# A fused attention and SoLU kernel: the row maximum by an accumulating multiply, the low half of x on VectorE, a group's first value product later

## The chip, the cores and the metric

The kernel runs on one core of one Trainium2 chip. The metric is the device time of one execution in microseconds (us), the median of several runs. TensorE (PE) multiplies matrices, VectorE (DVE), ScalarE (ACT) and GpSimd (POOL) work element by element, and SyncE (SP) issues most transfers. TensorE's results lie in PSUM, which GpSimd does not touch in this kernel.

## What is computed

```python
kv_flat = kv.reshape(B, H//4, 4, W//4, 4, C).mean(axis=(2, 4)).reshape(B, -1, C) @ w_sr   # k = v
s = q @ k.T / sqrt(C); a = softmax(s)              # 4 x 12288 queries, 768 keys, C = 128
x = a @ v                                          # 49152 tokens of 128
h = x @ w_in                                       # 1024 wide
u = h * softmax(h)
out = ((u - mean(u)) / sqrt(var(u) + 1e-6) * g_ln) @ w_out
```

Products are made as three products of split operands (a high half, and a low half that holds what the high half lost), so `x`, `k`, `v`, `q`, `u` and the weights all exist as two tiles each.

## The kernel before

The 49152 tokens are 384 **tiles** of 128; four tiles are a **group** (96 of them), and 96 tiles share one batch's keys. The main loop (L762) runs over slots. In slot `s` it works on the scores of tile `s`, on the hidden layer of tile `s-10` and `s-11`, and on the output product of tile `s-13`. From slot 9 on the order of instructions is written by hand: each engine executes its instructions in the order in which the loop emits them.

In one slot, in that order: `scores_exp` (L379: VectorE takes the negated maximum of the 768 scores in PSUM, ScalarE makes the exponential in place and then the high half `phl`), `hidden_u` (L499: VectorE, `u = h * rz * e` with an accumulated sum), the first part of `values` (one product `xa += v * pT`, L423), `scores_pe` of the next tile (L359, six products), GpSimd's steps, `hidden_var` on ScalarE, `hidden_max` and `hidden_bias` (L471 to L482: VectorE's negated maximum of the 1024 elements of `h`, then a multiply of this one column by the tile's `rz`), `hidden_exp` (L484: ScalarE, which needs that column), the rest of `values`, `scores_split` (L392: VectorE makes the low half of `phl`, and SyncE issues its transposing transfer into `pT`), `hidden_pe` (L460, six products into `h`), `final_pe` (L544, 24 products from `uT`), `hidden_turn` (L524: SyncE issues the transposing transfer of `u`'s halves into `uT`).

Three PSUM tiles (`ps_r`, L78) go round between scores and hidden tiles. The scores of the next tile take over the tile that `hidden_u` read, and `hidden_pe` takes over the tile that `scores_split` read in the same slot. One PSUM bank (`ps_x`, L79) holds `xa`, the value product of a whole group.

Once a group: 18 value products are spread over four slots (`values`, L405, shares 4, 5, 5, 4; in slots where a batch's key work needs TensorE, and in the slots of the same place in every batch, 0, 6, 6, 6). Then `values_out` (L427) lets ScalarE copy `xa` out twice, as 16 bits (`xh`) and as four bytes (`xf`). In the next slot, which is called slot 1 of the group below, `values_split` (L436) lets GpSimd subtract the two into `xl`, `values_norm` (L442) prepares the softmax sums on GpSimd, `values_recip` (L451) makes `rz` from them, and `final_out` (L574) writes an earlier group's result. GpSimd also splits `u` for every tile (L520, L521), and in most slots of batches 0 to 2 it adds up the next batch's keys (`kv_add`, L190, L201).

Of the kernel before, what the change touches and what calls it, by code (L numbers as in the profile page):

```python
# [11 lines left out]
F32 = mybir.dt.float32  # L12
F32R = mybir.dt.float32r
F16 = mybir.dt.float16
# [7 lines left out]
P = 128  # L22
# [9 lines left out]
GT = 4  # L32
# [20 lines left out]
def kernel(  # L53
# [70 lines left out]
    def kv_alloc(b):  # L124
        for n, w, dt, bufs in (
            ("kT", NK, F32, 1),
            ("ks", NK, F32, 1),
            ("kh", NK, F32R, 2),
            ("kl", NK, F32R, 2),
            ("ksq", NK, BF16, 1),  # L130
            ("kss", 2, F32, 1),
            ("knm", 2, F32, 1),
            ("vf", NK, F32, 1),
            ("sv", 2, F32, 2),
            ("bb", 4, F32, 2),
        ):
            state[n, b] = bat.tile([P, w], dt, tag=n, name=f"{n}_{b}", bufs=bufs)
        for n in ("vh", "vl"):
            state[n, b] = bat.tile([P, NKC, P], F16, tag=n, name=f"{n}_{b}")
# [125 lines left out]
    def kv_bound(b, part):  # L265

        knm, bb, sv = state["knm", b], state["bb", b], state["sv", b]  # L270
        if part == 0:
            nc.vector.tensor_tensor(knm[:, 0:1], knm[:, 0:1], knm[:, 1:2], op=ALU.max)
            nc.vector.tensor_scalar(
                bb[:, 0:1], knm[:, 0:1], wmax2, 1e-20, op0=ALU.mult, op1=ALU.max
            )
            nc.vector.tensor_scalar(knm[:, 0:1], knm[:, 0:1], 1e-28, None, op0=ALU.max)
            nc.gpsimd.tensor_tensor(bb[:, 0:1], bb[:, 0:1], mhalf[:, 0:1], op=ALU.pow)
            nc.gpsimd.tensor_tensor(knm[:, 0:1], knm[:, 0:1], mhalf[:, 0:1], op=ALU.pow)
        elif part == 1:
            nc.vector.tensor_scalar(  # L280
                bb[:, 1:2], bb[:, 0:1], SC * 1e-3 * 2.0**15, None, op0=ALU.mult
            )
            nc.vector.tensor_scalar(bb[:, 0:1], bb[:, 0:1], SC, None, op0=ALU.mult)
            nc.vector.tensor_scalar(bb[:, 2:3], bb[:, 1:2], 1e-9, None, op0=ALU.mult)
            pow2_under(knm[:, 0:1])
        else:
            nc.vector.tensor_scalar(knm[:, 0:1], knm[:, 0:1], 2.0**5, None, op0=ALU.mult)
            nc.vector.tensor_scalar(bb[:, 3:4], knm[:, 0:1], wsc, None, op0=ALU.mult)
            nc.vector.tensor_scalar(sv[:, 1:2], sv[:, 1:2], knm[:, 0:1], None, op0=ALU.mult)

    def kv_vs(b, half):
# [113 lines left out]
    def values(g, qtr, part):  # L405
        share = {0: [0, 0, 18, 0], 1: [0, 6, 6, 6]}.get(g, [4, 5, 5, 4])
        first = GT * g + GT - 1 + LAV
        if g > 1 and {first % TPB, first % TPB + TPB} & WITH_PE:
            share = [0, 6, 6, 6]
        s0 = sum(share[:qtr])  # L410
        s1 = s0 + share[qtr]
        if s0 == s1:
            return
        s0, s1 = ((s0, s0 + 1), (s0 + 1, s1))[part]
        b = g * GT // TPB
        if s0 == 0:
            state["xa", g] = ps_x.tile([P, 512], F32, tag="x", name=f"xa_{g}")
        xa, pT = state["xa", g], state["pT", g]
        vh, vl = state["vh", b], state["vl", b]
        seq = [(a, c, v) for c in range(NKC) for (a, v) in ((0, vh), (1, vh), (0, vl))]  # L420
        for n in range(s0, s1):
            a, c, v = seq[n]
            nc.tensor.matmul(  # L423
                xa, v[:, c, :], pT[:, :, a * NKC + c, :], start=n == 0, stop=n == len(seq) - 1
            )

    def values_out(g):  # L427
        b = g * GT // TPB
        xa, sv = state.pop(("xa", g)), state["sv", b][:, 1:2]
        xf = grp.tile([P, 512], F32, tag="xf", name=f"xf_{g}", bufs=1)  # L430
        xh = grp.tile([P, 512], F16, tag="xh", name=f"xh_{g}")
        nc.scalar.activation(xh, xa, AF.Copy, scale=sv)
        nc.scalar.activation(xf, xa, AF.Copy, scale=sv)
        state["xf", g] = (xf, xh)

    def values_split(g):  # L436
        xf, xh = state.pop(("xf", g))
        xl = grp.tile([P, 512], F16, tag="xl", name=f"xl_{g}")
        nc.gpsimd.tensor_tensor(xl, xf, xh, op=ALU.subtract)  # L439
        state["x", g] = (xh, xl)  # L440

    def values_norm(g):  # L442
        b = g * GT // TPB
        zz = grp.tile([P, GT], F32, tag="zz", name=f"zz_{g}", bufs=2)
        rz = grp.tile([P, 2, GT], F32, tag="rz", name=f"rz_{g}", bufs=3)
        nc.gpsimd.tensor_scalar(  # L446
            zz, state.pop(("z", g)), 1e-9, state["bb", b][:, 3:4], op0=ALU.add, op1=ALU.mult
        )
        state["zz", g] = (zz, rz)

    def values_recip(g):  # L451
        zz, rz = state.pop(("zz", g))
        nc.vector.reciprocal(rz[:, 0, :], zz)
        nc.scalar.activation(rz[:, 1, :], rz[:, 0, :], AF.Copy, scale=state["bb", g * GT // TPB][:, 0:1])  # L454
        state["rz", g] = (rz[:, 0, :], rz[:, 1, :])
        state["z2", g] = grp.tile([P, GT], F32, tag="z2", name=f"z2_{g}", bufs=3)
        state["v3", g] = grp.tile([P, GT], F32, tag="v3", name=f"v3_{g}", bufs=3)

# [10 lines left out]
        state["h", t] = h  # L469

    def hidden_max(t):  # L471
        g, j = divmod(t, GT)
        nm = wrk.tile([P, 2], F32, tag="nm2", name=f"nm2_{t}", bufs=3)
        nc.vector.tensor_reduce(nm[:, 0:1], state["h", t], axis=AX.X, op=ALU.max, negate=True)  # L474
        state["nm", t] = nm

    def hidden_bias(t):
        g, j = divmod(t, GT)
        nm = state["nm", t]
        nc.vector.tensor_scalar(  # L480
            nm[:, 1:2], nm[:, 0:1], state["rz", g][0][:, j : j + 1], None, op0=ALU.mult
        )  # L482

    def hidden_exp(t):  # L484
        g, j = divmod(t, GT)
# [4 lines left out]
            e,  # L490
            state["h", t],
            AF.Exp,
            bias=nm[:, 1:2],
            scale=state["rz", g][0][:, js],
            accum_out=state["z2", g][:, js],
        )
# [2 lines left out]
    def hidden_u(t):  # L499
# [3 lines left out]
        nc.vector.scalar_tensor_tensor(  # L503
            u,
            state.pop(("h", t)),
            state["rz", g][1][:, j : j + 1],
            state.pop(("e", t)),
            op0=ALU.mult,
            op1=ALU.mult,
# [239 lines left out]
    def at(t, fn, *args):  # L749
        if 0 <= t < NT:  # L750
            fn(t, *args)

    def at_last(t, fn, *args):

        if 0 <= t < NT and t % GT == GT - 1:
            fn(t // GT, *args)
# [5 lines left out]
    for slot in range(NT + LO + 2):  # L762
# [16 lines left out]
                st[0]()  # L779
        at(slot, scores_exp)  # L780
        at(i - 1, hidden_u)
        if 0 <= av < NG:
            values(av, qtr, 0)
        at(slot + 1, scores_pe)
        at_last(slot - NORM, values_norm)
        at_last(slot - XSP - 1, values_split)
        at_last(slot - FSC, final_scale)
        if slot < NT and 0 < qs < slot and (slot - 1 - qs) % GT == 0:
            q_low(slot // GT + 1)
        at(i - 1, hidden_split)  # L790
        at(i - 1, hidden_var)
        at(i, hidden_max)
        at(i, hidden_bias)
        at(i, hidden_exp)
        for f in fill.get(slot, []):
            f()
# [7 lines left out]
                f()  # L804
        at(slot, scores_split)
        at_last(slot - NORM, values_recip)
        at(i + 1, hidden_pe)
        at(slot - LO, final_pe)
        at(i - 1, hidden_turn)
# [43 lines left out]
```

## Time and profile before

| | us |
|---|---|
| median of 3 runs | 1930.72 |
| lowest, highest | 1929.51, 1938.44 |
| profiled execution | 1927.93 |
| its span | 1926.1 |
| PE busy | 1855.6 |
| ACT busy | 1803.2 |
| DVE busy | 1795.2 |
| POOL busy | 1705.3 |

An engine's busy time is the union of its instructions' spans. A matmul's end is modelled, so a busy PE may still be a PE that works below its rate. Instructions on one engine overlap at their ends: the next may start before the row of the one before it ends, so what an instruction costs its engine is the distance from its start to the next start, where nothing is waited for.

### The profile page before, as it was taken

How to read it: one execution, taken by the hardware profiler on the slowest of the kernel's cores; microseconds unless marked ns; L12 is line 12 of the kernel's file. 1: busy time of each engine (PE TensorE's matmuls, PEld its weight loads, DVE VectorE, ACT ScalarE, POOL GpSimd, SP SyncE). 2: the span in 40 equal slices, each digit the busy share in tenths (PEclk: the TensorE clock that was granted, in tenths of full speed). 3: DMA queues.
4: the chain of work that ended last, by engine and by line, in shares of the span. 5: the costliest groups of instructions: out<-in, count | busy, mean ns of one | idle time of the engine just before them, and what ended most of it. 6: DMA issues, size and time to landing. Idle time of an engine off the chain costs nothing. (4 is left out here: it accounts for less than half of the span.)

```text
span 1926.1 us, 43006 instructions
## 1 busy us (share of the span) xinstructions
PE 1855.6 (96%) x15677; PEld 1308.1 (68%) x15678; DVE 1795.2 (93%) x2600; ACT 1803.2 (94%) x3239; POOL 1705.3 (89%) x1392
## 2 busy tenths in 40 slices
PE   7899999999999999999999999999999999999996
PEld 4566776666766676766676767676677777776664
DVE  7998999999999898999999999999999999999985
ACT  4998999999999899999999999999999999999995
POOL 4698999988999989998989999998898988888886
PEclk8999999999999999999999999999999999999999
DMA  7899999999999999999999999999999999999996
GB/s 237 173 229 246 235 240 235 228 211 216 234 234 230 230 241 229 237 224 218 204 238 242 237 244 240 240 239 215 210 220 233 223 226 224 227 222 225 226 195 132
DMA packets 1484307, 432.85 MB, mean 225 GB/s; under 512 B 1405888, under 2 KB 1471552, under 8 KB 1483840
## 3 DMA queue, kind: packets, MB, share of 16 engines
q1 hardware_dynamic: 1469840, 410.10, 107.3%
q10 hardware_dynamic: 14256, 20.00, 4.0%
q8 instruction: 124, 2.03, 0.5%
q14 instruction: 87, 0.71, 0.1%
HBM read 52.50 MB, written 25.17 MB: 40 GB/s over the span
## 5 line engine op out<-in xcount | busy, mean ns | idle before, releaser
L521 POOL TENSOR_TENSOR uhl<-u,uhl 128x1024 f16<-128x1024 f32 x384 | 819.5, 2134 | 38.2 <-ACT uhl L518 6.7
L553 PEld LDWEIGHTS <-uT 128*128 128x128 f16 x9216 | 546.6, 98 | 109.1 <-DMA uT<-uhl 21.6
L553 PE MATMUL o<-wch,uT 128*128 128x128 f16 x6144 | 578.6, 220 | 14.9 <-DMA uT<-uhl 13.4
L553 PE MATMUL o<-wcl,uT 128*128 128x128 f16 x3072 | 535.7, 220 | 0.0
L503 DVE SCALAR_TENSOR_TENSOR u<-h,rz,e 128x1024 f32<-128x1024 f32 x384 | 491.1, 1279 | 29.2 <-ACT e L489 27.2
L474 DVE TENSOR_REDUCE nm<-h 128x1 f32<-128x1024 f32 x384 | 468.7, 1221 | 10.9 <-PE h L468 10.5
L489 ACT ACTIVATE e<-h,nm,rz 128x1024 f32<-128x1024 f32 x384 | 458.3, 1193 | 6.8 <-DVE nm L480 4.2
L534 ACT ACTIVATE junk<-u,su 128x1024 bf16<-128x1024 f32 x384 | 437.7, 1140 | 1.6 <-DVE u L503 1.6
L423 PE MATMUL xa<-pT,vh 128*128 128x512 f16 x1152 | 393.5, 383 | 16.8 <-ACT phl L389 5.5
L520 POOL TENSOR_SCALAR uhl<-u 128x1024 f16<-128x1024 f32 x378 | 394.7, 1044 | 7.2 <-DVE u L503 7.0
L397 DVE SCALAR_TENSOR_TENSOR phl<-s,phl 128x768 f16<-128x768 f32 x384 | 364.9, 950 | 26.7 <-ACT phl L389 17.1
L386 DVE TENSOR_REDUCE nm<-s 128x1 f32<-128x768 f32 x384 | 365.0, 951 | 24.3 <-PE s L370 22.8
L387 ACT ACTIVATE s<-s,nm 128x768 f32<-128x768 f32 x384 | 335.4, 873 | 38.5 <-DVE nm L386 37.7
L389 ACT ACTIVATE phl<-s 128x768 f16<-128x768 f32 x384 | 311.0, 810 | 12.0
L468 PEld LDWEIGHTS <-xh 128*128 128x128 f16 x1536 | 145.1, 98 | 205.7 <-DVE phl L397 41.9
L370 PE MATMUL s<-kh,qh 128*128 128x384 f32 x768 | 261.4, 421 | 10.9 <-DVE u L503 5.8
L468 PE MATMUL h<-w_in_h,xh 128*128 128x512 f16 x768 | 231.0, 383 | 13.7 <-DVE phl L397 7.3
L468 PE MATMUL h<-w_in_h,xl 128*128 128x512 f16 x768 | 230.0, 381 | 1.0 <-POOL xl L439 0.6
L468 PE MATMUL h<-w_in_l,xh 128*128 128x512 f16 x768 | 230.5, 382 | 0.0
L423 PE MATMUL xa<-pT,vl 128*128 128x512 f16 x576 | 220.1, 382 | 0.0
L370 PE MATMUL s<-kh,ql 128*128 128x384 f32 x768 | 197.9, 339 | 0.0
L370 PE MATMUL s<-kl,qh 128*128 128x384 f32 x768 | 195.4, 336 | 0.0
(130 smaller groups left out, 1997.6 us busy)
## 6 DMA issues: line engine op xcount, KB each, us to landing
qf<-in_q_dram SPq DMA_DIRECT2D x96, 256.0 KB, 3.3
out_dram<-ob SPq DMA_DIRECT2D x96, 256.0 KB, 3.1
kv<-in_kv_dram ACTq DMA_DIRECT2D x96, 192.0 KB, 3.6
kv<-in_kv_dram SPq DMA_DIRECT2D x16, 384.0 KB, 8.0
pT<-phl SPq DMA_TRANSPOSE x384, 4.0
uT<-uhl SPq DMA_TRANSPOSE x384, 4.5
raw_in<-in_moe_w_in_dram ACTq DMA_DIRECT2D x1, 1024.0 KB, 6.4
raw_out<-in_moe_w_out_dram SPq DMA_DIRECT2D x1, 1024.0 KB, 7.6
```

Source lines behind the costliest of these rows:

```text
L370: nc.tensor.matmul(s[:, half, :384], lh[:, ts], rh[:, half * 384 : (half + 1) * 384], start=n == 0, stop=n == 2,)
L386: nc.vector.tensor_reduce(nm, s, axis=AX.XY, op=ALU.max, negate=True)
L397: nc.vector.scalar_tensor_tensor(phl[:, 1], state.pop(("s", t)), SC, phl[:, 0], op0=ALU.mult, op1=ALU.subtract)
L423: nc.tensor.matmul(xa, v[:, c, :], pT[:, :, a * NKC + c, :], start=n == 0, stop=n == len(seq) - 1)
L468: nc.tensor.matmul(h[:, hs], lh[:, ts], rh[:, hs], start=n == 0, stop=n == 2)
L474: nc.vector.tensor_reduce(nm[:, 0:1], state["h", t], axis=AX.X, op=ALU.max, negate=True)
L489: nc.scalar.activation(e, state["h", t], AF.Exp, bias=nm[:, 1:2], scale=state["rz", g][0][:, js], accum_out=state["z2", g][:, js],)
L503: nc.vector.scalar_tensor_tensor(u, state.pop(("h", t)), state["rz", g][1][:, j : j + 1], state.pop(("e", t)), op0=ALU.mult, op1=ALU.mult, ...
L520: nc.gpsimd.tensor_scalar(uhl[:, 0, :], u, 1.0, 1.0, op0=ALU.mult, op1=ALU.mult)
L521: nc.gpsimd.tensor_tensor(uhl[:, 1, :], u, uhl[:, 0, :], op=ALU.subtract)
L534: nc.scalar.activation(junk, u, AF.Square, scale=-float(DFF), bias=su, accum_out=state["v3", g][:, j : j + 1],)
L553: nc.tensor.matmul(po[:, ts], uT[:, a * NFC + c, :], w[:, c, :], start=c == 0 and n == 0, stop=c == NFC - 1 and n == 2,)
```

## The change

- `hidden_max` no longer reduces `h` and then multiplies the result. One `tensor_scalar` multiplies all 1024 elements of `h` by a column of the negated reciprocal `-rz`, throws the product away into a bf16 tile, and accumulates the minimum. `hidden_bias` is gone.
- For that, `values_norm` makes two rows on GpSimd (with the factor and with its negative, a fifth column of `bb` that `kv_bound` fills once a batch), and `values_recip` takes the reciprocal of both at once.
- `values_out` keeps the 16-bit copy only. `values_split` is a `scalar_tensor_tensor` on VectorE that reads `xa` in PSUM, multiplies it by the same scale and subtracts `xh`. It stands right behind `hidden_u`.
- `values`: the first product of a group is no longer issued ahead of the next tile's scores; all of a group's first share goes behind them. Nothing changes for the other shares.

```diff
-            ("bb", 4, F32, 2),
+            ("bb", 5, F32, 2),
...
             nc.vector.tensor_scalar(bb[:, 3:4], knm[:, 0:1], wsc, None, op0=ALU.mult)
+            nc.vector.tensor_scalar(bb[:, 4:5], bb[:, 3:4], -1.0, None, op0=ALU.mult)
...
-        s0, s1 = ((s0, s0 + 1), (s0 + 1, s1))[part]
+        cut = s0 + (s0 > 0)
+        s0, s1 = ((s0, cut), (cut, s1))[part]
         b = g * GT // TPB
-        if s0 == 0:
+        if s0 == 0 and s1:
             state["xa", g] = ps_x.tile([P, 512], F32, tag="x", name=f"xa_{g}")
+        if s0 == s1:
+            return
...
     def values_out(g):
-        nc.scalar.activation(xh, xa, AF.Copy, scale=sv)
-        nc.scalar.activation(xf, xa, AF.Copy, scale=sv)
-        state["xf", g] = (xf, xh)
+        nc.scalar.activation(xh, state["xa", g], AF.Copy, scale=state["sv", b][:, 1:2])
+        state["x", g] = (xh, grp.tile([P, 512], F16, tag="xl", name=f"xl_{g}"))
 
     def values_split(g):
-        xf, xh = state.pop(("xf", g))
-        xl = grp.tile([P, 512], F16, tag="xl", name=f"xl_{g}")
-        nc.gpsimd.tensor_tensor(xl, xf, xh, op=ALU.subtract)
-        state["x", g] = (xh, xl)
+        xh, xl = state["x", g]
+        nc.vector.scalar_tensor_tensor(
+            xl,
+            state.pop(("xa", g)),
+            state["sv", g * GT // TPB][:, 1:2],
+            xh,
+            op0=ALU.mult,
+            op1=ALU.subtract,
+        )
...
-        nc.gpsimd.tensor_scalar(
-            zz, state.pop(("z", g)), 1e-9, state["bb", b][:, 3:4], op0=ALU.add, op1=ALU.mult
-        )
+        for k in range(2):
+            nc.gpsimd.tensor_scalar(
+                zz[:, k, :], z, 1e-9, bb[:, 3 + k : 4 + k], op0=ALU.add, op1=ALU.mult
+            )
...
-        nc.vector.reciprocal(rz[:, 0, :], zz)
-        nc.scalar.activation(rz[:, 1, :], rz[:, 0, :], AF.Copy, scale=state["bb", g * GT // TPB][:, 0:1])
+        nc.vector.reciprocal(rz[:, 0:2, :], zz)
+        state["rz", g] = [rz[:, k, :] for k in range(3)]
+
+    def values_recip_u(g):
+        rz = state["rz", g]
+        nc.scalar.activation(rz[2], rz[0], AF.Copy, scale=state["bb", g * GT // TPB][:, 0:1])
...
     def hidden_max(t):
-        nc.vector.tensor_reduce(nm[:, 0:1], state["h", t], axis=AX.X, op=ALU.max, negate=True)
+        nm = wrk.tile([P, 1], F32, tag="nm2", name=f"nm2_{t}", bufs=3)
+        junk = wrk.tile([P, DFF], BF16, tag="junkd", name=f"junkd_{t}", bufs=1)
+        nc.vector.tensor_scalar(
+            junk,
+            state["h", t],
+            state["rz", g][1][:, j : j + 1],
+            None,
+            op0=ALU.mult,
+            op1=ALU.min,
+            accum_out=nm,
+        )
-
-    def hidden_bias(t):
-        nc.vector.tensor_scalar(
-            nm[:, 1:2], nm[:, 0:1], state["rz", g][0][:, j : j + 1], None, op0=ALU.mult
-        )
...
         at(i - 1, hidden_u)
+        at_last(slot - XSP - 1, values_split)
         if 0 <= av < NG:
             values(av, qtr, 0)
         at(slot + 1, scores_pe)
         at_last(slot - NORM, values_norm)
-        at_last(slot - XSP - 1, values_split)
...
-        at(i, hidden_bias)
...
         at_last(slot - NORM, values_recip)
+        at_last(slot - NORM, values_recip_u)
```

## Rows read from the trace of the kernel before

**Rows 1.** The page's first part: busy us (share of the span) x instructions.
```profile
PE 1855.6 (96%) x15677; PEld 1308.1 (68%) x15678; DVE 1795.2 (93%) x2600; ACT 1803.2 (94%) x3239; POOL 1705.3 (89%) x1392
```

**Rows 2.** Windows: stretch us, PE, PEld, DVE, ACT, POOL busy (x), PEclk, DMA share, GB/s.
```profile
129.56:362.96 233.40, 227.88 (x1947) 161.18 (x1945) 219.66 (x312) 223.17 (x402) 221.56 (x182) 0.99 1.20 237
...
482.68:834.39 351.71, 341.95 (x2920) 242.44 (x2919) 329.19 (x469) 333.84 (x600) 326.94 (x267) 0.99 1.19 234
...
953.39:1297.15 343.76, 338.81 (x2919) 241.34 (x2918) 328.64 (x469) 333.17 (x600) 326.58 (x266) 1.00 1.20 239
1297.15:1416.43 119.28, 116.02 (x985) 81.09 (x983) 114.03 (x174) 113.64 (x208) 105.39 (x90) 1.00 1.09 212
1416.43:1752.79 336.36, 335.49 (x2915) 240.75 (x2914) 326.96 (x469) 330.55 (x595) 296.98 (x235) 1.00 1.15 227
```

**Rows 3.** Windows, L386 alone (one a tile): stretch us, DVE busy (x), clock, DMA.
```profile
1416.43:1752.79 336.36, 68.37 (x72) 1.00 1.15 227
```

**Rows 4.** Windows: a stall's aftermath, and one group of the last batch; columns as rows 2.
```profile
666.40:671.20 4.80, 4.79 (x16) 2.46 (x17) 2.16 (x3) 2.70 (x6) 4.21 (x4) 0.64 1.19 269
1640.93:1659.59 18.66, 18.66 (x164) 13.41 (x163) 18.18 (x28) 18.37 (x34) 16.51 (x14) 1.00 1.06 227
```

**Rows 5.** Timeline, VectorE, group slots 1 and 2: start us, us, engine, line, operation.
```profile
1645.38 0.96 DVE L386 TENSOR_REDUCE nm<-s 128x1 f32<-128x768 f32 x1
1646.26 1.28 DVE L503 SCALAR_TENSOR_TENSOR u<-h,rz,e 128x1024 f32<-128x1024 f32 x1
...
1647.46 1.22 DVE L474 TENSOR_REDUCE nm<-h 128x1 f32<-128x1024 f32 x1
...
1649.07 0.96 DVE L397 SCALAR_TENSOR_TENSOR phl<-s,phl 128x768 f16<-128x768 f32 x1
...
1650.02 0.72 DVE L577 SCALAR_TENSOR_TENSOR ob<-o,swi,f 128x512 f32<-128x512 f32 x1
1650.66 0.95 DVE L386 TENSOR_REDUCE nm<-s 128x1 f32<-128x768 f32 x1
1651.53 1.27 DVE L503 SCALAR_TENSOR_TENSOR u<-h,rz,e 128x1024 f32<-128x1024 f32 x1
...
1652.73 1.22 DVE L474 TENSOR_REDUCE nm<-h 128x1 f32<-128x1024 f32 x1
...
1654.11 0.95 DVE L397 SCALAR_TENSOR_TENSOR phl<-s,phl 128x768 f16<-128x768 f32 x1
```

**Rows 6.** Timeline, TensorE, the same slots: a score product, hidden products, the next scores.
```profile
1648.51 0.70 PE L370 MATMUL s<-kh,qh 128*128 128x384 f32 x2
...
1650.40 0.59 PE L468 MATMUL h<-w_in_h,xh 128*128 128x512 f16 x2
1650.84 0.60 PE L468 MATMUL h<-w_in_l,xh 128*128 128x512 f16 x2
...
1653.07 0.70 PE L370 MATMUL s<-kh,qh 128*128 128x384 f32 x2
```

**Rows 7.** Timeline, TensorE, a slot 1 without value products [idle before <-releaser].
```profile
1610.51 0.59 PE L370 MATMUL s<-kh,qh 128*128 128x384 f32 x2
...
1612.22 0.59 PE L468 MATMUL h<-w_in_h,xh 128*128 128x512 f16 x2 [0.44 <-ACT junk L534]
```

**Rows 8.** Groups by line, whole span: busy us, mean ns | idle before, releaser.
```profile
L439 POOL TENSOR_TENSOR xl<-xf,xh 128x512 f16<-128x512 f32 x96 | 111.3, 1159 | 13.2 <-ACT xf L433 6.5
...
L201 POOL TENSOR_TENSOR ka<-ka,kv 128x384 f32<-128x384 f32 x84 | 84.7, 1008 | 0.0
...
L433 ACT ACTIVATE xf<-xa,sv 128x512 f32<-128x512 f32 x96 | 65.4, 681 | 0.0
...
L446 POOL TENSOR_SCALAR zz<-z,bb 128x4 f32<-128x4 f32 x96 | 25.7, 267 | 11.9 <-DVE bb L288 2.3
...
L107 DVE TENSOR_SCALAR ex_out<-ex_out 128x1024 int32<-128x1024 int32 x1 | 0.7, 694 | 0.0
```

**Rows 9.** Waits of TensorE's weight loads, 482.68 to 834.39 us: total, times, longest.
```profile
PEld L423 <- DMA pT<-phl: 4.3, 2, 3.0
```

More of the change, by code (lines that the diff above doesn't have):

```diff
@@ L428, in values_out @@
         b = g * GT // TPB
-        xa, sv = state.pop(("xa", g)), state["sv", b][:, 1:2]
-        xf = grp.tile([P, 512], F32, tag="xf", name=f"xf_{g}", bufs=1)
         xh = grp.tile([P, 512], F16, tag="xh", name=f"xh_{g}")
-        nc.scalar.activation(xh, xa, AF.Copy, scale=sv)
-        nc.scalar.activation(xf, xa, AF.Copy, scale=sv)
-        state["xf", g] = (xf, xh)
+        nc.scalar.activation(xh, state["xa", g], AF.Copy, scale=state["sv", b][:, 1:2])
+        state["x", g] = (xh, grp.tile([P, 512], F16, tag="xl", name=f"xl_{g}"))
     def values_split(g):
-        xf, xh = state.pop(("xf", g))
-        xl = grp.tile([P, 512], F16, tag="xl", name=f"xl_{g}")
-        nc.gpsimd.tensor_tensor(xl, xf, xh, op=ALU.subtract)
-        state["x", g] = (xh, xl)
+        xh, xl = state["x", g]
[7 more added lines that the diff above has]
+        )
     def values_norm(g):
         b = g * GT // TPB
-        zz = grp.tile([P, GT], F32, tag="zz", name=f"zz_{g}", bufs=2)
-        rz = grp.tile([P, 2, GT], F32, tag="rz", name=f"rz_{g}", bufs=3)
-        nc.gpsimd.tensor_scalar(
-            zz, state.pop(("z", g)), 1e-9, state["bb", b][:, 3:4], op0=ALU.add, op1=ALU.mult
-        )
+        zz = grp.tile([P, 2, GT], F32, tag="zz", name=f"zz_{g}", bufs=2)
+        rz = grp.tile([P, 3, GT], F32, tag="rz", name=f"rz_{g}", bufs=3)
+        z, bb = state.pop(("z", g)), state["bb", b]
+        for k in range(2):
+            nc.gpsimd.tensor_scalar(
+                zz[:, k, :], z, 1e-9, bb[:, 3 + k : 4 + k], op0=ALU.add, op1=ALU.mult
+            )
         state["zz", g] = (zz, rz)
@@ L452, in values_recip @@
         zz, rz = state.pop(("zz", g))
-        nc.vector.reciprocal(rz[:, 0, :], zz)
-        nc.scalar.activation(rz[:, 1, :], rz[:, 0, :], AF.Copy, scale=state["bb", g * GT // TPB][:, 0:1])
-        state["rz", g] = (rz[:, 0, :], rz[:, 1, :])
+        nc.vector.reciprocal(rz[:, 0:2, :], zz)
[3 more added lines that the diff above has]
+        nc.scalar.activation(rz[2], rz[0], AF.Copy, scale=state["bb", g * GT // TPB][:, 0:1])
         state["z2", g] = grp.tile([P, GT], F32, tag="z2", name=f"z2_{g}", bufs=3)
@@ L472, in hidden_max @@
         g, j = divmod(t, GT)
-        nm = wrk.tile([P, 2], F32, tag="nm2", name=f"nm2_{t}", bufs=3)
-        nc.vector.tensor_reduce(nm[:, 0:1], state["h", t], axis=AX.X, op=ALU.max, negate=True)
-        state["nm", t] = nm
-    def hidden_bias(t):
-        g, j = divmod(t, GT)
-        nm = state["nm", t]
-        nc.vector.tensor_scalar(
-            nm[:, 1:2], nm[:, 0:1], state["rz", g][0][:, j : j + 1], None, op0=ALU.mult
-        )
+        nm = wrk.tile([P, 1], F32, tag="nm2", name=f"nm2_{t}", bufs=3)
[9 more added lines that the diff above has]
+        )
+        state["nm", t] = nm
     def hidden_exp(t):
@@ L492, in hidden_exp @@
             AF.Exp,
-            bias=nm[:, 1:2],
+            bias=nm,
             scale=state["rz", g][0][:, js],
@@ L505, in hidden_u @@
             state.pop(("h", t)),
-            state["rz", g][1][:, j : j + 1],
+            state["rz", g][2][:, j : j + 1],
             state.pop(("e", t)),
```

## The prediction

> **What bounds the kernel now.** I read the busy times first: four engines are busy 89 to 96% of the span [rows 1], so the shares alone name no bound. The windows by stage do. In the last batch 72 tiles [rows 3] take 336.36 us, 4.67 us a tile, and TensorE is busy for 335.49 of them [rows 2]; one group of four tiles there takes 18.66 us with TensorE busy for all of it, VectorE for 18.18 and ScalarE for 18.37 [rows 4]. Its matmuls follow each other without a hole, so this is TensorE's **floor**: no relief of another engine can make a group shorter than 18.66 us. What can be won is what the other stages take above it.
>
> In the three stages in which GpSimd also gathers the next batch's keys, 48, 72 and 72 tiles take 233.40, 351.71 and 343.76 us [rows 2]. At the floor they would take 224.2, 336.4 and 336.4: they are 9.2, 15.4 and 7.4 us over, 31.9 together. TensorE is idle in them for 5.5, 9.8 and 5.0 us (length less busy), 20.2 together. Some of the rest is a slow clock: after the longest stall the granted clock was 0.64 over 4.8 us [rows 4], between 2.4 and 1.2 GHz, which costs 4.8 x 0.36 = 1.7 us. The first two of these stages show a mean clock of 0.99, which is 2.3 and 3.5 us of slow clock. The remaining 8 us are the keys' own products. The stage between gathering and the next batch (24 tiles, one of three like it) takes 119.28 us, 7.2 over the floor, with TensorE idle for 3.3 [rows 2].
>
> What TensorE waits for while keys are gathered: GpSimd is busy 326.58 us in 72 tiles, 18.14 a group, 97% of the floor, against 296.98 or 16.50 a group (88%) in the last batch, where TensorE hardly waits [rows 2]. A GpSimd that runs late makes the halves of `u` late, SyncE waits for them and holds the next transposition of the scores behind them, and the first value product of a group waits for that: two weight loads for it wait 4.3 us for the transfer into `pT`, the longer one 3.0 [rows 9].
>
> **Part by part.** *The maximum.* Before, a reduction and a small multiply: from L474 to L397 is 1654.11 - 1652.73 = 1.38 us where nothing is waited for [rows 5]. After, one multiply with an accumulated minimum. No row shows this operation. From below, a `tensor_scalar` of 1024 four-byte elements in SBUF took 0.69 us [rows 8]; from above, the two instructions it replaces, 1.38. The nearest row is L503: same 1024 elements from PSUM, an accumulated result, and 1647.46 - 1646.26 = 1.20 us to the next start, its accumulator's row included [rows 5]. I take 1.20, a saving of 0.18 a tile. The Trainium skill, "VectorE: DVE Perf Modes", section "Why PSUM operands drop a tier", says that a four-byte operand in PSUM keeps VectorE at one element a cycle; by that the lower end is out of reach, and no run here shows it yet.
>
> *xl on VectorE.* It is 512 elements from PSUM, as L577 is: 0.72 us, 0.64 to the next start [rows 5]. I take 0.64 a group, all in slot 1. VectorE's group is then 4 x 0.18 = 0.72 shorter and 0.64 longer: as good as unchanged, but **slot 1 is 0.46 us longer and the others 0.18 shorter**. The reciprocal of 8 instead of 4 columns I cost at nothing: four more elements, hidden in VectorE's slack of 0.5 a group [rows 4]; without that cover a few ns.
>
> *Does the longer slot 1 still fit?* Counted from L386 at 1645.38 in rows 5: L503 at +0.88, `xl` at +2.08, the maximum at +2.72, L397 at +3.92 = 1649.30 (before 1649.07), done at 1650.26. `hidden_pe`, which takes over its PSUM tile, starts at 1650.40 [rows 6]: 0.14 us to spare. Reciprocal and L577 as before, so the next L386 starts 0.23 later, L503 at 1651.76, done at 1653.03; the next scores, which take over that tile, start at 1653.07 [rows 6]: 0.04 to spare. In slots 2, 3 and 0 VectorE gains 0.18 each and catches up. `xl` is done near 1648.2; the value products that reuse its bank now come behind the scores that start at 1648.51 [rows 6], so that wait is covered by more than a us, and `xh` is ScalarE's job of before. So at the floor nothing is won and nothing lost, by a narrow margin.
>
> *Slots without value products* (24 groups, of which 6 in the last batch): `hidden_pe` follows the scores at once and already waits 0.44 us [rows 7], by the rows' order for L397. That comes 0.23 later: +0.2 us where no key products fill the hole, about 10 groups, **+2**.
>
> *ScalarE* loses `xf`, 0.68 us a group [rows 8]: slack, for it is not the bound. *GpSimd* loses `xl`, 1.16, and gains a second `zz`, 0.27 [rows 8]: -0.89 a group. In the gathering stages 18.14 becomes 17.25, 92% of the floor. The extra column of `bb` is four instructions in all, nothing.
>
> *The first value product later.* A product ahead of the scores lies partly in their start-up: the first pair of score products takes 0.70 with it [rows 6] and 0.59 without [rows 7]. So it costs 0.11 plus two starts of about 0.03 each there, and all of its 512 columns behind the scores, 0.22 (half the distance of two pairs of that width, 1650.40 to 1650.84 [rows 6]): +0.05 a group, 94 groups, **+5**. In return the transfer has the time of the six scores more, about 1.2 us (1648.51 to 1650.40, less three value products of 0.22 [rows 6]). The wait of 3.0 becomes 1.8, and the other, 1.3, all but vanishes.
>
> *Gathering stages.* GpSimd at 92% lies between 97% (20.2 us idle) and 88% (0.9 idle in 72 tiles, 2.3 in 192 [rows 2]). Straight between them would leave about 10; the later first product takes another us off each stall. I leave 4.5: -16, and 4 of the slow clock's 6 us with the long stalls: **-20**. *Stages between:* VectorE's small key steps fall partly into slot 1, so the longer slot costs 0.2 to 0.4 in some of them, against 0.18 won per tile elsewhere: **+2** (-5 to +6). *Start and end:* there the chain from `xa` over `xf` and `xl` to `h` runs bare, and loses 0.68 of ScalarE and about 0.4 of GpSimd against VectorE for three groups at the end and a few at the start: **-4**.
>
> Sum: +2 +5 -20 +2 -4 = -15, on the profiled execution's 1927.9 (span 1926.1): 1913. That execution lies 2.8 under the median of the runs shown, 1930.7. So I forecast 1915.
>
> **The rivals.** *All stalls go.* The 20.2 us of idle and 6 of slow clock vanish, and ScalarE's slack takes 5 more out of the stages between: -6 -5 on the forecast and about -5 at the start: 1899. For it: all that GpSimd held back has one cause. Against: transfers run at 239 GB/s while keys are gathered, 227 otherwise [rows 2], and late landings may have their own reason.
>
> *The transfers are the limit.* Then GpSimd's relief changes nothing; only the later product helps, 1.2 off each of some 7 stalls of which two are in rows 9, 8 us, less its own 5, +2 +2 and -4: 1927.9 - 3, with the 2.8 a time of 1928. For it: the same 239 GB/s. Against: the last batch at 227 shows hardly any stall, and the worst stalls begin with SyncE behind GpSimd.
>
> *VectorE becomes the bound, slower.* If the maximum costs as much as the pair, VectorE's group is 0.64 longer: about 18.7, all of the floor, and slot 1's margins of 0.14 and 0.04 turn into a wait of some 0.2 to 0.3 in every group: 25 us, and 3 more where no value products stand: 1943. It decides from 1.23 us a maximum on (0.04 of margin). For it: no row shows the operation. Against: L503, the same size with the same accumulator row. A page's rule would go further: the Trainium skill, "VectorE: DVE Perf Modes", section "The DRAIN you can't avoid", says that after every operation the next waits until the pipe is empty, so that only the rows' full durations count. By it `xl` would cost its full 0.72 a group and the maximum save next to nothing, up to 68 us in 94 groups. The trace disagrees: L503's row lasts 1.28 and the next starts 1.20 after it [rows 5]. I give it 0.01, within this rival.
>
> That the change doesn't do what it says is only possible in the small: the minimum could leave a second row that is not hidden, which is this rival again.
>
> **How the numbers follow.** Forecast 0.55 (own range 1903 to 1924), all stalls go 0.13, transfers 0.18, VectorE 0.14. A measurement of this kernel tells about 0.5% from no change, that is 9.7 us: faster below 1921, slower above 1940. Faster: 0.47 of the forecast, all of 0.13, 0.02 of the transfers: 0.62. Slower: 0.11 of VectorE's case, 0.02 for what I haven't seen: 0.13. Same: 0.25. The range from 1897 to 1938 takes in the forecast, the transfers and most of the case without stalls, and leaves the worst of VectorE's out.
>
> **What would show it.** Right: the maximum's row near 1.25 us with an accumulator row behind it and 1.20 to the next start; `xl` near 0.7 on VectorE; the last batch at 336 to 341 us; the gathering stages 5 to 8 us shorter each, GpSimd near 92% and no TensorE wait of 2 us ahead of a value product. Wrong: a maximum of 1.3 us or more; score products that wait for `u` in slot 2 of every group, or hidden products for L397; idle TensorE in the gathering stages as before, waiting for `uT` or `pT`; a last batch above 345 us.

## Result and profile after

The median fell from 1933.6 to 1913.6 us (four runs each, 1907.7 to 1920.5 after); the ratio is 0.9896, 95% interval 0.987 to 0.9922. Measured again beside other kernels it is 0.9893 (0.9862 to 0.9925). The forecast was 1915, so the time came out. Its largest terms did not.

The profiled execution of the changed kernel took 1920.5 us (span 1918.7), the slowest of its four. Its busy times, as in [rows 1]:

```profile
PE 1855.9 (97%) x15678; PEld 1306.6 (68%) x15678; DVE 1793.5 (93%) x2700; ACT 1760.2 (92%) x3143; POOL 1624.6 (85%) x1392
```

VectorE is as busy as before, ScalarE 43 us and GpSimd 81 us less; the rows removed alone are 65.4 us, and 111.3 less 25.7 added [rows 8]. TensorE has the same work. Where its time went is in the windows by stage, cut at the same tiles as [rows 2]; columns as there (stretch us, PE, PEld, DVE, ACT, POOL busy (x), clock, DMA share, GB/s):

```profile
128.15:361.21 233.06, 226.97 (x1946) 160.03 (x1945) 219.89 (x325) 217.81 (x390) 211.41 (x183) 1.00 1.21 237
361.21:478.05 116.84, 115.31 (x985) 81.64 (x983) 112.23 (x180) 110.83 (x202) 99.98 (x89) 1.00 1.10 219
478.05:823.88 345.83, 340.46 (x2919) 240.69 (x2917) 329.00 (x486) 325.06 (x582) 311.73 (x267) 1.00 1.21 237
823.88:940.71 116.83, 115.28 (x985) 81.63 (x983) 112.24 (x180) 110.82 (x202) 99.97 (x89) 1.00 1.13 220
940.71:1292.97 352.26, 342.90 (x2919) 241.09 (x2917) 329.84 (x486) 325.66 (x582) 311.60 (x267) 0.99 1.19 234
1292.97:1409.79 116.82, 115.27 (x985) 81.61 (x983) 112.24 (x180) 110.83 (x202) 99.96 (x89) 1.00 1.06 216
1409.79:1747.64 337.85, 336.48 (x2915) 239.49 (x2913) 328.24 (x486) 323.12 (x577) 282.40 (x235) 1.00 1.14 225
```

The three stages between gathering and the next batch went from 119.0 to 119.7 us each to 116.8 each. The last batch went from 336.36 to 337.85. The gathering stages are 233.06, 345.83 and 352.26: against 4.672 us a tile they lie 8.8, 9.5 and 15.9 us over the floor, 34.2 together, where the profile of before had 31.9. So in this execution nothing was won where the prediction looked for most of the gain, although GpSimd's load there fell as forecast (311.73 us in 72 tiles, 17.3 a group; before 18.14).

The table gives for each kernel of this document its time as a ratio to the kernel before, measured beside it, and what its profiles show by the same cut: the three gathering stages over the floor (192 tiles at 4.672 us), the three stages between over the floor (72 tiles), the last batch's 72 tiles, and the rest of the span (start and end).

| kernel | ratio to before (95%) | gathering, over | between, over | last batch | rest |
|---|---|---|---|---|---|
| before | 1 | 31.9 | 21.6 | 336.4 | 302.9 |
| before, second profile | | 36.4 | 21.4 | 336.4 | 301.7 |
| after | 0.9896 (0.987 to 0.9922) | 34.2 | 14.1 | 337.9 | 299.2 |
| after, second profile | 0.9893 (0.9862 to 0.9925) | 26.2 | 14.1 | 337.9 | 299.4 |
| first product later alone | 1.0008 (0.9981 to 1.0034) | 33.4 | 22.8 | 337.4 | 303.8 |
| xl on VectorE alone | 0.9992 (0.9965 to 1.002) | 24.2 | 21.2 | 343.3 | 303.9 |
| maximum alone | 0.9957 (0.9936 to 0.9978) | 29.5 | 16.1 | 336.4 | 300.6 |
| after, first product as before | 0.9884 (0.9838 to 0.9931) | 24.7 | 12.3 | 337.3 | 298.9 |
| after, few key transfers | 0.9774 (0.9716 to 0.9833) | 4.5 | 14.2 | 337.9 | 299.1 |
| after, few key additions | 0.9883 (0.9822 to 0.9943) | 28.0 | 14.2 | 337.9 | 299.5 |
| after, output one slot later | 0.9939 (0.9914 to 0.9964) | 33.4 | 12.1 | 337.7 | 297.3 |
| before, few key transfers | 0.9859 (0.9829 to 0.9889) | 15.0 | 20.8 | 336.4 | 300.6 |
| before, few key additions | 1.0004 (0.9981 to 1.0027) | 42.6 | 20.8 | 336.4 | 301.1 |
| after, key transfers halved | 0.9801 (0.9776 to 0.9825) | 16.2 | 14.1 | 337.9 | 298.7 |

From one profile of a kernel to the next the last batch repeats to 0.1 us and the stages between to 0.3; the gathering stages do not, by 4.5 us before and 8 after. That is where runs of the same kernel differ, and a gathering figure of a single profile has to be read with that spread in mind.

### The profile page after: what moved, and what is told of

Same layout as the page of the kernel before. It is cut to its first block, busy times and chain, and to the rows that moved or that the text cites. A ratio compares the mean times of both kernels' runs of the same rounds, so it can differ in the third digit from the quotient of the medians.

```text
span 1918.7 us, 43085 instructions
## 1 busy us (share of the span) xinstructions
PE 1855.9 (97%) x15678; PEld 1306.6 (68%) x15678; DVE 1793.5 (93%) x2700; ACT 1760.2 (92%) x3143; POOL 1624.6 (85%) x1392
## 5 line engine op out<-in xcount | busy, mean ns | idle before, releaser
L518 DVE SCALAR_TENSOR_TENSOR u<-h,rz,e 128x1024 f32<-128x1024 f32 x384 | 491.0, 1279 | 30.0 <-ACT e L504 12.6
L488 DVE TENSOR_SCALAR_CACHE_REDUCE junkd<-h,rz 128x1024 bf16<-128x1024 f32 x384 | 491.3, 1279 | 14.5 <-PE h L480 13.2
L387 DVE TENSOR_REDUCE nm<-s 128x1 f32<-128x768 f32 x384 | 365.3, 951 | 50.1 <-PE s L371 44.5
L427 PE MATMUL xa<-pT,vh 128*128 128x512 f16 x1152 | 377.0, 382 | 14.1 <-issue 3.6
L398 DVE SCALAR_TENSOR_TENSOR phl<-s,phl 128x768 f16<-128x768 f32 x384 | 366.0, 953 | 5.8 <-ACT phl L390 5.8
L371 PE MATMUL s<-kh,qh 128*128 128x384 f32 x768 | 256.0, 414 | 8.4 <-DVE u L518 3.9
```

The lines of the kernel that those rows point to most:

```text
L371: nc.tensor.matmul(s[:, half, :384], lh[:, ts], rh[:, half * 384 : (half + 1) * 384], start=n == 0, stop=n == 2,)
L387: nc.vector.tensor_reduce(nm, s, axis=AX.XY, op=ALU.max, negate=True)
L398: nc.vector.scalar_tensor_tensor(phl[:, 1], state.pop(("s", t)), SC, phl[:, 0], op0=ALU.mult, op1=ALU.subtract)
L427: nc.tensor.matmul(xa, v[:, c, :], pT[:, :, a * NKC + c, :], start=n == 0, stop=n == len(seq) - 1)
L488: nc.vector.tensor_scalar(junk, state["h", t], state["rz", g][1][:, j : j + 1], None, op0=ALU.mult, op1=ALU.min, accum_out=nm,)
L518: nc.vector.scalar_tensor_tensor(u, state.pop(("h", t)), state["rz", g][2][:, j : j + 1], state.pop(("e", t)), op0=ALU.mult, op1=ALU.mult, ...
```

## The steady group, row by row

VectorE in the changed kernel, slots 1 and 2 of a group in the last batch; columns as [rows 5]:

```profile
1639.96 0.96 DVE L387 TENSOR_REDUCE nm<-s 128x1 f32<-128x768 f32 x1 [0.43 <-PE s L371]
1640.84 1.28 DVE L518 SCALAR_TENSOR_TENSOR u<-h,rz,e 128x1024 f32<-128x1024 f32 x1
1642.04 0.09 DVE L518 DVE_READ_ACCUMULATOR u<-h,rz,e 128x1 f32 x1
1642.04 0.75 DVE L439 SCALAR_TENSOR_TENSOR xl<-xa,sv,xh 128x512 f16<-128x512 f32 x1
1642.70 1.28 DVE L488 TENSOR_SCALAR_CACHE_REDUCE junkd<-h,rz 128x1024 bf16<-128x1024 f32 x1
1643.90 0.09 DVE L488 DVE_READ_ACCUMULATOR junkd<-h,rz 128x1 f32 x1
1643.90 0.95 DVE L398 SCALAR_TENSOR_TENSOR phl<-s,phl 128x768 f16<-128x768 f32 x1
...
1645.49 0.95 DVE L387 TENSOR_REDUCE nm<-s 128x1 f32<-128x768 f32 x1
1646.36 1.27 DVE L518 SCALAR_TENSOR_TENSOR u<-h,rz,e 128x1024 f32<-128x1024 f32 x1
```

TensorE in the same slots, as [rows 6]:

```profile
1643.03 0.59 PE L371 MATMUL s<-kh,qh 128*128 128x384 f32 x2
...
1645.03 0.59 PE L480 MATMUL h<-w_in_h,xh 128*128 128x512 f16 x2
...
1647.70 0.69 PE L371 MATMUL s<-kh,qh 128*128 128x384 f32 x2
```

The new maximum lasts 1.28 us and the next instruction starts 1.20 after it, exactly L503's distance in [rows 5]; its accumulator's row lies under the next instruction. `xl` costs 0.66. L398 starts 3.94 us after L387 (forecast 3.92) and ends at 1644.85, 0.18 before the hidden products that need its PSUM tile; L518 of slot 2 ends at 1647.63, 0.07 before the scores that need its tile. The margins are about as narrow as they were forecast, 0.14 and 0.04, and they hold: TensorE waits for VectorE in neither slot.

Where slot 1 has no value products, the hidden products wait longer than in [rows 7], 0.69 instead of 0.44:

```profile
1604.63 0.59 PE L371 MATMUL s<-kh,qh 128*128 128x384 f32 x2
...
1606.60 0.59 PE L480 MATMUL h<-w_in_h,xh 128*128 128x512 f16 x2 [0.69 <-DVE rz L462]
```

The row names the reciprocal, L462, but the products follow the end of L398 (1606.45) by 0.15 us, as they followed L397's by 0.14 in the kernel before (1612.08 to 1612.22). It is the wait for L398 that was forecast.

## Experiments

**The changed kernel once more.** No edit.

> The changed kernel once more, for a second profile. In the first one the three gathering stages together lay 34.2 us above the floor (before 32.0), the stages between 14.1 (before 21.5). Theory GpSimd (its lateness makes the stalls of the gathering stages): these 34.2 were a bad execution; this one shows 12 to 18. Theory transfers (SyncE's queue and its transposing transfers make them): 25 to 36 again, with TensorE waiting for uT and pT. Both: the stages between at 13 to 15, the median at 0.985 to 0.995 of the kernel before.

It measured 1911.7 us. The gathering stages, windows with the columns of above:

```profile
127.93:359.72 231.79, 227.84 (x1946) 161.74 (x1945) 219.58 (x325) 217.55 (x390) 211.54 (x183) 0.99 1.20 238
...
476.54:817.96 341.42, 338.79 (x2919) 239.84 (x2917) 328.77 (x486) 325.02 (x582) 311.80 (x267) 1.00 1.21 241
...
934.78:1284.69 349.91, 340.90 (x2919) 240.88 (x2917) 329.41 (x486) 325.64 (x582) 311.67 (x267) 1.00 1.20 235
```

26.2 us over the floor: in the range of the theory that blames the transfers, far from the 12 to 18 of GpSimd's. The stages between lie at 14.1 again.

**One part at a time.** The first product alone:

```diff
-        s0, s1 = ((s0, s0 + 1), (s0 + 1, s1))[part]
+        cut = s0 + (s0 > 0)
+        s0, s1 = ((s0, cut), (cut, s1))[part]
...
```

> The kernel before, with the first value product of a group behind the scores and nothing else. Theory GpSimd: the waits ahead of that product shrink by 1.2 us each, -8, and the product costs 0.05 a group, +5: 0.998 of before, last batch 340 us instead of 336. Theory transfers: the same late transfers are then waited for at uT instead, so -2 to 0 in the gathering stages and +5: 1.001 to 1.003.

Ratio 1.0008, gathering 33.4, last batch 337.36 and not 340. The price of 0.05 us a group is there (1.0 us in 18 groups); the gain is not.

`xl` on VectorE alone, with `values_out` and `values_split` as in the change and `values_split` behind `hidden_u`:

```diff
...
-        nc.scalar.activation(xf, xa, AF.Copy, scale=sv)
...
-        nc.gpsimd.tensor_tensor(xl, xf, xh, op=ALU.subtract)
+        nc.vector.scalar_tensor_tensor(
+            xl, state.pop(("xa", g)), sv, xh, op0=ALU.mult, op1=ALU.subtract
+        )
```

> The kernel before, with the low half of x made by VectorE and the four-byte copy gone; the maximum and the first value product as before. VectorE's group becomes 18.04 + 0.66 = 18.7 us, as long as the floor, and slot 1 0.66 us longer. Theory GpSimd: the gathering stages fall from 32 to 15 us above the floor, but a wait of 0.2 to 0.4 us a group for VectorE costs 20 to 30: 1.00 to 1.01 of before. Theory transfers: the gathering stages keep their 32: 1.01 to 1.02. Both: the last batch at 340 to 345 us.

The first gathering stage (48 tiles), the second (72) and the last batch:

```profile
129.19:364.44 235.25, 229.54 (x1946) 161.31 (x1945) 225.40 (x325) 219.24 (x390) 208.20 (x170) 0.99 1.20 236
...
484.61:827.52 342.91, 341.86 (x2919) 239.91 (x2917) 335.63 (x487) 328.05 (x582) 307.55 (x249) 1.00 1.18 240
...
1407.84:1751.09 343.25, 340.59 (x2915) 239.19 (x2913) 335.76 (x487) 326.63 (x577) 277.90 (x217) 1.00 1.10 222
```

The last batch is 6.9 us longer: VectorE is now the bound, 335.8 us busy of 343. At that slower pace the two gathering stages of 72 tiles take no longer than the last batch, and TensorE is idle for 1.1 us of each. The first, of 48 tiles, has its stalls as before: TensorE is idle for 5.7 us. The ratio of 0.9992 fits the GpSimd theory's lower end, 1.00; the 24.2 us over the floor lie between its 15 and the other's 32. So the stalls are not a fixed toll, and a slower pace may hide them, but this one profile does not show that it always does.

The maximum alone:

```diff
-        nc.vector.tensor_reduce(nm[:, 0:1], state["h", t], axis=AX.X, op=ALU.max, negate=True)
+        nc.vector.tensor_scalar(
+            junk, state["h", t], state["rz", g][1][:, j : j + 1], None,
+            op0=ALU.mult, op1=ALU.min, accum_out=nm,
+        )
...
```

> The kernel before, with the accumulating maximum of h (and its second row from GpSimd) alone. VectorE saves 0.18 us a tile, GpSimd pays 0.3 a group. Both theories: the stages between, where TensorE waits for VectorE, fall from 21.5 to about 14 us above the floor, the last batch stays at 336. Theory GpSimd: the gathering stages get 3 to 6 us worse, 0.998 of before. Theory transfers: they stay near 32, 0.994 to 0.996.

Ratio 0.9957. A gathering stage, a stage between and the last batch:

```profile
943.77:1290.55 346.78, 339.67 (x2918) 241.13 (x2917) 320.24 (x469) 334.13 (x600) 331.48 (x285) 1.00 1.19 237
1290.55:1408.04 117.49, 115.86 (x986) 81.25 (x984) 108.95 (x174) 113.45 (x208) 107.41 (x95) 1.00 1.10 217
1408.04:1744.44 336.40, 335.52 (x2915) 241.39 (x2914) 317.75 (x469) 330.73 (x595) 302.03 (x253) 1.00 1.13 226
```

GpSimd is busier than before, 331.48 us against 326.58, and the gathering stages are no worse (29.5 over the floor): the theory of the transfers forecast that, the other one 3 to 6 us more. The stage between went from 119.28 to 117.49, and the last batch did not move. Its gain is 0.43%, that of `xl` 0.08%, that of the place -0.08%, and all three make 1.07%. Together the parts give more than their sum because `xl` needs the time that the maximum frees: alone it makes VectorE the bound. In the last batch the three alone cost 0, 6.9 and 1.0 us, all together 1.5.

**The first product put back into the changed kernel.**

```diff
-        cut = s0 + (s0 > 0)
-        s0, s1 = ((s0, cut), (cut, s1))[part]
+        s0, s1 = ((s0, s0 + 1), (s0 + 1, s1))[part]
```

> The changed kernel with the first value product of a group back ahead of the scores; maximum and low half of x as in the changed kernel. That product waits for the low half of x, which VectorE finishes near +2.8 us of slot 1, and stands at +3.1 there. If its place matters only through the 0.05 us a group: 0.985 of before, last batch 336.5. If the 1.2 us that the pT transfer gains matter: the gathering stages get 8 us worse, 0.992 to 0.995. If TensorE waits for the low half of x: the last batch above 340 and 1.00.

0.9884 with an interval that holds the changed kernel's ratio. Neither the 8 us of loss nor a wait for `xl` shows (last batch 337.3). Nothing of the move's gain can be measured. Its price can, in the stages that repeat: with the old place the stages between lie 1.8 us lower and the last batch 0.6 (table).

**Transfers or GpSimd.** Two kernels take one of them away in the gathering stages; their keys of batches 1 to 3 are then incomplete. Without 14 of 16 key transfers of each half batch, so that GpSimd adds the same two slices again and again:

```diff
...
+        if pos > 1:
+            return
         r, two = divmod(pos, 2)
...
-        t = state["kv", b, half, pos // 2]
+        t = state["kv", b, half, 0]
```

> The changed kernel without 14 of 16 key transfers of each half batch: GpSimd adds the same two slices again and again, so its work is all there, and the keys of batches 1 to 3 are not the reference's. Theory transfers: the three gathering stages fall from 26 to 34 us above the floor to under 12 (their own products are 5, the later first product 4), with SyncE's instructions back near 84% of the stage. Theory GpSimd: they stay at 25 or more.

Two gathering stages and the last batch:

```profile
470.41:808.26 337.85, 337.78 (x2919) 240.29 (x2917) 328.12 (x486) 325.27 (x582) 311.79 (x267) 1.00 1.15 228
925.11:1263.08 337.97, 337.90 (x2919) 240.22 (x2917) 328.02 (x486) 325.52 (x582) 311.84 (x267) 1.00 1.14 228
1379.94:1717.79 337.85, 336.49 (x2915) 239.59 (x2913) 328.11 (x486) 323.74 (x577) 282.30 (x235) 1.00 1.13 225
```

GpSimd is as busy as in the changed kernel, 311.8 us, and TensorE is idle for 0.07 us in 338. Every stall of the gathering stages is gone; 4.5 us over the floor are left. Without 13 of 15 additions of each half batch:

```diff
-        nc.gpsimd.tensor_tensor(state["ka", b, half], x, t[:, pos % 2, :], op=ALU.add)
+        if pos % 8 == 1:
+            nc.gpsimd.tensor_tensor(state["ka", b, half], x, t[:, pos % 2, :], op=ALU.add)
```

> The changed kernel with all key transfers, but with 2 of 15 additions a half batch on GpSimd, so the keys of batches 1 to 3 are not the reference's. GpSimd falls to its load of the last batch. Theory transfers: the gathering stages keep 20 us or more above the floor, with TensorE waiting for uT and pT. Theory GpSimd: they fall under 12.

```profile
476.15:822.27 346.12, 339.14 (x2919) 240.29 (x2917) 329.41 (x486) 326.08 (x582) 287.31 (x241) 1.00 1.19 237
939.12:1287.06 347.94, 339.77 (x2919) 239.86 (x2917) 329.26 (x486) 326.29 (x582) 287.38 (x241) 1.00 1.21 236
```

GpSimd is down to 287 us and TensorE idle for 7.0 and 8.2: 28.0 over the floor. In the changed kernel the key transfers make the stalls, and of GpSimd's additions no part shows beyond the spread of 8 us. The same two edits on the kernel before tell what its stalls were made of:

> The kernel before without 14 of 16 key transfers of each half batch (same additions on the same two slices, keys of batches 1 to 3 not the reference's). GpSimd keeps its 97% of the floor in the gathering stages. If the transfers alone made those stages' 32 us, they fall to under 10. If GpSimd's lateness made a part of it, as the prediction said, 12 to 20 stay.

> The kernel before with all key transfers and 2 of 15 additions a half batch (keys of batches 1 to 3 not the reference's): GpSimd falls from 97% to under 92%, as the change does. If GpSimd's lateness made the stalls of the gathering stages, they fall from 32 to under 15 us above the floor; if the transfers made them, they stay at 22 or more.

```profile
481.20:835.01 353.81, 340.86 (x2920) 241.78 (x2919) 329.14 (x469) 333.71 (x600) 302.63 (x241) 1.00 1.21 233
954.03:1306.49 352.46, 340.26 (x2920) 242.89 (x2919) 329.27 (x469) 334.01 (x600) 302.81 (x241) 1.00 1.20 233
```

Those rows are of the kernel with few additions: GpSimd fell from 327 to 303 us and the stages are 42.6 us over the floor, no better than with its full load; the ratio is 1.0004. With few transfers and GpSimd's full load they are 15.0 over, in the range that the expectation gave to GpSimd's lateness as a part. So before, too, the transfers made most of it. GpSimd's share can show only where they are gone: 15.0 against 4.5 with the change, and that difference holds the other parts' effect as well.

**A slot more for the output.**

```diff
-LO = 13
+LO = 14
...
-        uT = dmt.tile([P, 2 * NFC, P], F16, tag="uT", name=f"uT_{t}", bufs=4)
+        uT = dmt.tile([P, 2 * NFC, P], F16, tag="uT", name=f"uT_{t}", bufs=5)
```

> The changed kernel with the output products one slot later (14 instead of 13) and a fifth buffer for uT, so the transfer of u has 4.7 us more. If the gathering stages' waits for uT are a matter of latency (a transfer now and then late), most of their 15 us vanish and the stages lie 12 to 18 us above the floor together; 0.982 to 0.985 of before. If SyncE's queue or the transfers are short of throughput, the wait moves to pT or stays, and nothing is won: 0.988 to 0.992.

Waits of TensorE's weight loads from 100 to 1860 us (total, times, longest), the changed kernel first:

```profile
PEld L568 <- DMA uT<-uhl: 20.3, 28, 2.0
...
PEld L427 <- DMA pT<-phl: 5.8, 10, 1.7
```

```profile
PEld L427 <- DMA pT<-phl: 13.1, 10, 3.7
...
PEld L427 <- DMA kv<-in_kv_dram: 4.0, 4, 2.9
```

The waits for `uT` are gone and come back as longer waits for `pT`. 33.4 over the floor, 0.9939 against 0.9893: nothing is won, and some 8 us seem lost. The later first product moved waits as well. In the same stretch the kernel before has load waits of 11.3 us for `uT` and 5.7 for `pT`; with the later product alone they are 18.4 and 7.3, in the changed kernel 20.3 and 5.8, and in the changed kernel with the old place 11.6 and 8.0. Using `pT` later made the waits for `uT` longer.

**The key transfers in halves.** Each key transfer of 192 KB (one every second slot) becomes two of 96 KB, one a slot:

```diff
         nc.scalar.dma_start(
-            state["kv", b, half, r][:, two, :], kv[b - 1, r, :, k0 : k0 + 384]
+            state["kv", b, half, r][:, two, :192], kv[b - 1, r, :, k0 : k0 + 192]
         )
+    def kv_load_rest(b, part):
...
+            state["kv", b, half, r][:, two, 192:], kv[b - 1, r, :, k0 + 192 : k0 + 384]
...
+    PLAN += [(5 + 2 * r - 2 * (r // RR), r, kv_load_rest) for r in range(2 * RR)]
```

> The changed kernel with each key transfer of 192 KB cut in two of 96 KB, the second one slot later, so that every slot carries the same bytes; more instructions on ScalarE's queue, all else the same. If bursts (a key transfer beside one of q and two transpositions) make the late transfers, the gathering stages fall from 26 to 34 to under 20 us above the floor, 0.982 to 0.986 of before. If it is the bytes, they stay: 0.988 to 0.991.

```profile
474.18:817.35 343.17, 339.29 (x2919) 239.65 (x2917) 328.78 (x486) 325.43 (x582) 312.39 (x267) 1.00 1.21 239
934.18:1274.39 340.21, 338.40 (x2919) 239.88 (x2917) 328.40 (x486) 324.69 (x582) 311.88 (x267) 1.00 1.22 241
```

1897.7 us, 0.9801 (0.9776 to 0.9825), the fastest of the kernels here that do all the work, and its runs differ less (1896.1 to 1902.4). The gathering stages are 16.2 us over the floor with the same bytes moved. So it is largely a matter of how the bytes are bunched, and not of how many there are; a smaller transfer and an even spacing were not tried apart. Nor is it the issuing on ScalarE, of which this kernel has twice as much. The 11.7 us that still separate it from the kernel with few transfers (16.2 - 4.5) were not taken apart.

**The kernel before once more.** No edit.

> The kernel before once more, for a second profile of its stages. Its first profile was of an execution of 1927.9 us, its median over the runs is 1933 to 1936. If the stages outside the gathering ones repeat to a few tenths (21.5 us above the floor between, 336.4 in the last batch) and the gathering ones make the spread, this execution shows them at 32 us plus what it lasts longer than 1927.9, so 35 to 42 at the median. If the spread lies elsewhere, they stay at 32.

1931.1 us, 3.2 more than its first profiled execution; gathering 36.4, 4.5 more; all else within 1.2 us. The spread lies in the gathering stages.

## One stall, followed through the rows

The longest stall of TensorE in the main loop of the changed kernel's profile. SyncE's and ScalarE's issues (start, us, engine, line), then TensorE:

```profile
1253.21 0.57 SPq L340 DMA_DIRECT2D qf<-in_q_dram  x1
1253.88 1.73 SPq L401 DMA_TRANSPOSE pT<-phl  x1
1255.78 5.01 SPq L541 DMA_TRANSPOSE uT<-uhl  x1
1260.89 1.43 SPq L401 DMA_TRANSPOSE pT<-phl  x1
```

```profile
1254.48 0.35 ACTq L186 DMA_DIRECT2D kv<-in_kv_dram  x1
```

```profile
1257.66 0.51 PE L371 MATMUL s<-kh,ql 128*128 128x384 f32 x2
1261.42 1.01 PE L427 MATMUL xa<-pT,vh 128*128 128x512 f16 x2 [3.25 <-issue]
```

Three transfers are issued within 1.3 us: 256 KB of `q`, the scores' transposition of a group's last tile, and a key transfer. By the trace's landing marks (a transfer's end) the key transfer, with a median of 4.0 us to landing, took 6.6 and landed at 1261.10; the transposition, with a median of 4.4 in this stage, landed at 1261.33, 7.5 us after its issue, and TensorE went on at 1261.42. The row's "issue" is thus a wait for that landing. Why the transfers were late is not shown: in those 3.25 us they moved 149 GB/s, less than the stage's 234. After the stall the granted clock was 0.50, that is 1.2 GHz:

```profile
1261.20:1265.40 4.20, 3.98 (x10) 1.50 (x11) 0.30 (x2) 2.06 (x5) 3.52 (x3) 0.50 1.62 259
```

It stayed at 0.50 until 1267.31. TensorE was busy at half speed for 5.89 us, which cost by estimate 2.9 us more, nearly the wait over again.

The longest stall of the kernel before has the same three transfers in the same order:

```profile
659.84 0.57 SPq L339 DMA_DIRECT2D qf<-in_q_dram  x1
660.50 1.28 SPq L400 DMA_TRANSPOSE pT<-phl  x1
660.95 0.40 ACTq L186 DMA_DIRECT2D kv<-in_kv_dram  x1
666.41 0.39 PE L423 MATMUL xa<-pT,vh 128*128 128x512 f16 x1 [2.88 <-ACT rz L454]
```

The key transfer landed at 665.79, the transposition at 666.37, 5.9 us after its issue, and TensorE went on at 666.41. GpSimd's part in it is at most small: L397, which makes the transposition's operand, ended at 660.02, and the issue of `pT` began 0.48 us later, behind that of `q`. The rest is the transfer's own time. All nine waits of more than 1 us in the gathering stages of that profile end 0.04 to 0.09 us after a transposition's landing, and so do all six of the changed kernel; these transpositions took 4.9 to 8.3 us, where the medians in the last batches are 3.9 to 4.1.

Median times to landing in the third gathering stage, `uT`: the changed kernel, and the one with few key transfers:

```profile
uT<-uhl SPq DMA_TRANSPOSE x72, 5.0
```

```profile
uT<-uhl SPq DMA_TRANSPOSE x72, 4.1
```

SyncE issues in order, so a late issue holds the next: that of `uT` at 1255.78 lasted 5.01 us, and the next `pT`'s began at 1260.89. From the end of VectorE's L398 to the end of SyncE's issue row of that `pT` the median is 5.3 us in this stage of the changed kernel, 2.2 with few key transfers and 1.9 in the last batch (worked out from 72 pairs of rows each).

## Why the prediction was right in sum, and where it was wrong

*The floor, the maximum, slot 1:* right to a few hundredths, as shown above. The price of the maximum was the largest unknown; the nearest row, L503, gave it exactly. VectorE as a new bound, the slower rival, is real but one step away: it is the kernel with `xl` alone.

*The first product, +5 and some of the -20:* the price was about right (0.05 a group alone, 0.03 in the changed kernel), the gain was not there. The step that failed is "the later first product takes another us off each stall". A later use of `pT` moves the wait; as long as the transfers come late, TensorE meets them at the next thing it needs, here `uT` (11 to 12 us of load waits without the move, 17 to 20 with it).

*Gathering stages, -20:* wrong in cause. The step that failed is the line drawn from 97% to 88% of GpSimd's load. The last batch differs from the gathering stages in two things, additions and key transfers, and the line put all of the difference down to the first. The rows had shown the second as well (234 to 239 against 227 GB/s [rows 2]), and it was only a rival. Nor does the longest stall before begin with SyncE behind GpSimd, as the prediction says of the worst ones: `pT` was issued half a us after its operand was done, and 5.9 us went into the transfer. Taking GpSimd's additions away moved nothing beyond the spread; taking the transfers away moved 17 to 21 of 32 to 36 us before and 22 to 30 after. The split of the 32 was off as well: 20.2 of idle and 5.8 of slow clock leave 6 for the keys' own products, not 8, and 4.5 were left where the stalls were gone. Of the prediction's signs of being wrong one came: TensorE idles in the gathering stages as before, for 20.8 and 15.6 us in the two profiles (20.2 before), and waits for `uT` and `pT`.

What the change did win here can only be bounded: the profiles show 31.9 and 36.4 before, 34.2 and 26.2 after. The medians fell by 20 to 21 us, of which the other stages explain 9 (7.4 between, 3.0 at start and end, less 1.5 in the last batch; before is the mean of two profiles here and below), which would leave some 12 for the gathering stages; that is an inference from medians, not read in a profile. The same reckoning leaves about 12 for `xl` alone (4 us faster, though the other stages cost 8) and nothing for few additions on the kernel before. So that gain, if it is one, came with `xl` and not through GpSimd's load; its cause stays open.

*Stages between, +2:* wrong in sign, and outside the -5 to +6 that it was given; they gave -7.4. There TensorE waits for VectorE, and the term set 0.2 to 0.4 us for a longer slot 1 against the 0.18 of each of 24 tiles without adding up the latter, 4.3 us a stage. The maximum alone gave -5.4, `xl` alone -0.3, all three parts -7.4, and without the later product -9.2.

*Start and end, -4:* measured -3 (302.9 and 301.7 became 299.2 and 299.4). *Slots without value products, +2:* the wait grew by 0.25 where 0.2 was said; the last batch, together with the later product, took 1.5 us more.

*The rivals:* the transfers as the limit was right about what makes the stalls of the gathering stages, wrong that the later product shortens them, and wrong in its total of 1928, in large part since it too had +2 for the stages between. That 1915 was met is luck: a gain that was too large by about 8 us stood beside one that was missed by 9. The forecast also started from a median of 1930.7; from the 1933.6 of four runs the change is -20 us, where about -16 was forecast.

## What to carry over

A stage that is worse than another differs from it in everything that runs there: before a stall is put down to the busiest engine, look for what else is only there, the transfers first, and test by taking each away. When an operand comes late because of transfers, using it later only moves the wait; cutting a burst of 192 KB into two of 96 KB a slot apart brought nearly as much again (0.989 to 0.980) as the whole change had (1 to 0.989). And two changes on one engine belong together when one spends what the other frees: alone, `xl` made VectorE the bound.

## What the hardware showed unexpectedly

A `tensor_scalar` with an accumulated result on 1024 elements in PSUM runs as its own operation, 1279 ns a row as L503, with an 83 ns accumulator row that costs nothing where the next instruction is ready. The Trainium skill, "VectorE: DVE Perf Modes", section "Why PSUM operands drop a tier", keeps a four-byte operand in PSUM at the slowest mode, and its "Specifications" give the engine's clock as 0.96 GHz. By that page's clock one element a cycle is an estimated 1.04 ns an element. The rows agree: `xl` with 512 elements takes 0.66 us from start to start and L488 with 1024 takes 1.20, 1.05 ns for each further element. The wait for the pipe to empty, which the same page states in "The DRAIN you can't avoid", does not show: L518's row lasts 1.28 and the next starts after 1.20, as the page's remark there on a next instruction that isn't held would have it.

A transposition's time to landing depends on what else is in flight: in the third gathering stage the median of `uT` is 5.0 us beside the key transfers and 4.1 with most of them left out, and TensorE's idle time in 72 tiles falls from between 2.6 and 9.4 us (two profiles) to 0.07. The same bytes in transfers of half the size, one a slot, leave 1.8 to 3.9.
